# Placing the transposes and the averages of the second attention stage between the two tiles of a block

## The chip, the cores and the metric

The kernel runs on one core of one Trainium2 chip. The metric is the device time of one execution in microseconds (us), as the median of the runs shown. Engines: PE is TensorE, DVE VectorE, ACT ScalarE, POOL GpSimd, SP SyncE, which here issues all DMAs.

## What is computed

Two layers, each an attention block A and a dense block B, with a residual sum around each; 2048 rows of 640 numbers, 32 heads of 20, fp32. The reference, cut to what matters:

```python
def _A_ref(x, wqkv, w_phi, wo):
    q, k, v = split_heads(x @ wqkv)
    pq, pk = q @ w_phi, k @ w_phi                     # per head
    phi_q = concat([softmax(pq), softmax(-pq)])       # 40 features a head
    phi_k = concat([softmax(pk), softmax(-pk)])
    kv = phi_k.T @ v                                  # sum over all rows
    z = phi_k.sum(over rows)
    o = (phi_q @ kv) / (phi_q @ z + 1e-6)
    return merge_heads(o) @ wo
def _B_ref(x, w1, b1, w2):
    h = x @ w1 + b1
    return mish(h) @ w2
for _ in range(2):
    x = x + _A_ref(layernorm(x), ...)
    x = x + _B_ref(layernorm(x), ...)
```

The sum `kv` needs all rows before the first output row can be made. So each layer's attention has two stages.

## The kernel before, in words

The 2048 rows are cut into 8 blocks (NB) of 256 rows, each of two tiles of 128 rows (BT = 2). Products that must be exact in fp32 are made of three products each: every operand is held as a high part and a low part, and high x high, high x low and low x high are added up.

**First stage** (`attend_first`): features of keys and queries and the values of each block; `kv` grows in PSUM over all blocks. The features of the queries are written to DRAM, one tensor `e_d[b]` for each block, turned (L421 to L425), in pieces of 128 bytes; the pieces of the last block are still open when the second stage begins. They sit in a generator, `rest`, and each call of `tail()` (L552) takes one step of it.

**Second stage** (`attend_second`, L547), the one that is changed. For each block b:

- `load(b)` (L517) reads the turned features back: two DMAs of 600 KB into two "big" tiles (L521; there are 5 such buffers) and one of 80 KB into an "ol" tile (L523). In the code after, `phi(b)` does the same.
- `average(b, t)` (L557) makes `o` for tile t: 44 small products on PE (L567) into one `mm_tile` (two PSUM banks; there are two such tiles), then VectorE divides (L576 to L580) into a `row_tile` (tag "xn", 4 buffers).
- `Transposed(rows).all()` (L263) turns the two row tiles of a block: 10 transposes on PE (L278) in three steps, each into a `one_tile` (one PSUM bank; there are four). ScalarE copies the high part out, VectorE subtracts to get the low part (L284).
- `Rows(b, t).half(c, ps)` (L594) is half of the output product `o @ wo` for tile t: 15 products of 320 columns (L342) into the bank `ps`, then VectorE adds the block's input rows x to it (L597) and takes statistics (L598).
- `norm_scale` (L253) makes scale and offset for the layer norm that follows, on GpSimd and VectorE. The block's result, which lies in the tile of x, is stored (L649).
- `fetch(x_src, b + 1)` (L380) reads the next block's x. There are two x tiles.
- `makes[b]` and `fetches[b + 1]` prepare the weights of the dense stage: reads on SP (L141), a copy on ScalarE, a subtraction on GpSimd (L149).

**What sets the order.** For PE and SP the order in this stage is the written one (`manual_schedule`, L605). For the other engines a planner orders the instructions of the whole kernel by its own model of times. Waits between engines come from the use of tiles: a buffer that is given out again waits until its last reader has finished, and two halves written into one `mm_tile` belong to one tile.

**The written order of a block before**, for 1 <= b <= 6: average(b+1, 0); half 0 of tile 0; average(b+1, 1); tail; read of x(b+1); load(b+3); half 1 of tile 0; half 0 of tile 1; transposes of block b+1; half 1 of tile 1; store; reads of weights; tail. Tile 0's halves use one `one_tile` each; tile 1's lie in the two banks of one `mm_tile`, `py`. Ahead of the loop stand the averages of blocks 0 and 1 and loads 1 to 3; in the last block the transposes of the dense stage's first rows (`ahead.all()`) stand in front.

**Dense stage** (`dense`): both products with Mish between them, its PE order made by the planner.

Of the kernel before, what the change touches and what calls it, by code (L numbers as in the profile page):

```python
# [24 lines left out]
BT = 2  # L25
BLK = BT * P
NB = S // BLK
# [15 lines left out]
def kernel(  # L43
# [22 lines left out]
    def mm_tile():  # L66
        return psum.tile([P, 2, 512], F32, tag="mm", name="mm", bufs=2)

    def one_tile():
        return psum.tile([P, 512], F32, tag="one", name="one", bufs=4)  # L70

    def big_tile():
        return work.tile([P, EW], F32, tag="big", name="big", bufs=5)
# [4 lines left out]
    def pair_tile(dtype=F32R):  # L78
        return work.tile([P, 2, BLK], dtype, tag="ol", name="ol", bufs=6)

    def row_block(t, b):
        return t[b * BLK:(b + 1) * BLK, :].rearrange("(p t) d -> p t d", t=BT)
# [211 lines left out]
    def row_tile():  # L294
        return work.tile([P, D], F32, tag="xn", name="xn", bufs=4)
# [40 lines left out]
    def project_half(ps, xts, t, ws, col, c, ks=range(KD)):  # L336
        sl = slice(t * P, (t + 1) * P)
        cs = slice(col + c * HC, col + (c + 1) * HC)
        for k in ks:
            h, l, wh, wl = xts.hs[k], xts.ls[k], ws[k][0][:, cs], ws[k][1][:, cs]  # L340
            for n, (a, r) in enumerate(((h, wh), (h, wl), (l, wh))):
                nc.tensor.matmul(ps[:, :HC], a[:, sl], r, start=(k == 0 and n == 0),  # L342
                                 stop=(k == KD - 1 and n == 2))
# [36 lines left out]
    def fetch(x_src, b, xt=None):  # L380
        xt = x_tile() if xt is None else xt
        nc.sync.dma_start(xt, row_block(x_src, b))
        return xt
# [133 lines left out]
    def load(b):  # L517

        ta, tb, tc_ = big_tile(), big_tile(), pair_tile(F32)
        for t, g0 in ((ta, 0), (tb, 5)):  # L520
            nc.sync.dma_start(t[:120].rearrange("f (g s) -> f g s", s=BLK),  # L521
                              e_d[b][120 * g0:120 * (g0 + 5)].rearrange("(g f) s -> f g s", f=120))
        nc.sync.dma_start(tc_[:80, 0], e_d[b][1200:])  # L523
        return [(ta, tb)[g // 5][:, (g % 5) * BLK:(g % 5 + 1) * BLK] for g in range(10)] + [tc_[:, 0]]

    def finish_kv(kva, kvz, mask):

        acc, acz = row_tile(), row_tile()
        for src, dst, p1, n, w in ((kva, acc, P, 4, 120), (kvz, acz, P, 1, 120), (kvz, acz, 42, 1, 80)):
            c = 120 if w == 80 else 0  # L530
            nc.vector.tensor_tensor(dst[:p1, c:c + n * w].rearrange("p (n w) -> p n w", n=n),
                                    src[:p1, c:c + n * w].rearrange("p (n w) -> p n w", n=n),
                                    mask[:p1, :w].unsqueeze(1).to_broadcast([p1, n, w]), op=ALU.mult)
        yield
        for src, q0, n in ((acc, 0, 4), (acz, 4, 2)):
            ps = one_tile().rearrange("p (n c) -> p n c", n=4)
            for q in range(n):
                p1, w = (P, 120) if q0 + q < 5 else (42, 80)
                nc.tensor.transpose(ps[:w, q, :p1], src[:p1, 120 * q:120 * q + w], ident[:p1, :p1])
            if n == 4:  # L540
                act(kvb[:, :4], ps[:120], AF.Copy)
            else:
                nc.vector.tensor_copy(kvb[:, 4], ps[:120, 0])
                nc.vector.tensor_copy(kvb[:80, 5, :42], ps[:80, 1, :42])
        yield

    def attend_second(x_src, x_dst, acc, fetches, makes, fetch_next, begin_next):  # L547
        kva, kvz, o_ws, loaded, rest = acc
        rows = {}
        div = [None]  # L550

        def tail():  # L552

            with tc.issue_after(div[0]):
                next(rest, None)

        def average(b, t):  # L557

            phs = loaded[b]
            po = mm_tile()  # L560
            for g in range(G):
                n = 120 if g < 10 else 80
                w = GW if g < 10 else 42
                c, j = divmod(g, 8)
                for q in range(2):
                    s0 = t * P + 64 * q
                    nc.tensor.matmul(  # L567
                        po[64 * q:64 * q + 64, c, GW * j:GW * j + w], phs[g][:n, s0:s0 + 64],
                        kvb[:n, g // 2, 64 * (g % 2):64 * (g % 2) + w], start=True, stop=True)
            o = row_tile()  # L570
            den = work.tile([P, H], F32, tag="r", name="den", bufs=2)
            pv = [po[:, c, :(DH + 1) * n].rearrange("p (h d) -> p h d", d=DH + 1)
                  for c, n in ((0, 24), (1, 8))]
            hh = (slice(0, 24), slice(24, H))
            for c in range(2):
                nc.vector.tensor_scalar_add(den[:, hh[c]], pv[c][:, :, DH], DEN_EPS)  # L576
            nc.vector.reciprocal(den, den)
            for c in range(2):
                n = hh[c].stop - hh[c].start
                ins = nc.vector.tensor_tensor(o.rearrange("p (h d) -> p h d", d=DH)[:, hh[c]], pv[c][:, :, :DH],  # L580
                                        den[:, hh[c]].unsqueeze(2).to_broadcast([P, n, DH]), op=ALU.mult)
                div[0] = ins.ins
            rows.setdefault(b, []).append(o)
            if t == BT - 1:
                del loaded[b]

        class Rows:


            def __init__(self, b, t):  # L590
                self.t, self.xt, self.ps = t, xs[b], None
                self.bn = work.tile([P, 2, 6], F32, tag="bn", name="bn", bufs=2)

            def half(self, c, ps):  # L594
                project_half(ps, cur, self.t, o_ws, 0, c)
                part = self.xt[:, self.t, c * HC:(c + 1) * HC]
                nc.vector.tensor_tensor(part, ps[:, :HC], part, op=ALU.add)  # L597
                nc.vector.bn_stats(self.bn[:, c], part)  # L598

            def mean(self):  # L600
                mv = work.tile([P, 2], F32, tag="mv", name="mv", bufs=3)
                nc.vector.bn_aggr(mv, self.bn)
                return mv

        with tc.manual_schedule(engines={mybir.EngineType.PE, mybir.EngineType.SP}):  # L605
            kv = finish_kv(kva, kvz, mask)
            next(rest)
            next(kv)
            loaded[1] = load(1)
            xs = {0: fetch(x_src, 0)}  # L610
            fetches[0]()
            next(rest)
            next(kv)
            next(rest)
            average(0, 0)
            average(0, 1)
            loaded[2] = load(2)
            average(1, 0)
            cur = Transposed(rows.pop(0)).all()
            average(1, 1)  # L620
            loaded[3] = load(3)
            for b in range(NB):
                if b == NB - 1:
                    ahead.all()
                elif b:
                    average(b + 1, 0)
                r0, r1 = Rows(b, 0), Rows(b, 1)
                r0.half(0, one_tile())
                if 0 < b < NB - 1:
                    average(b + 1, 1)  # L630
                tail()
                if b + 1 < NB:
                    xs[b + 1] = fetch(x_src, b + 1)
                if 0 < b and b + 3 < NB:
                    loaded[b + 3] = load(b + 3)
                if b == NB - 3:
                    fetch_next()
                r0.half(1, one_tile())
                mv0 = r0.mean()
                if b == NB - 2:  # L640
                    ahead = begin_next()
                py = mm_tile()
                r1.half(0, py[:, 0])
                if b + 1 < NB:
                    nxt = Transposed(rows.pop(b + 1)).all()
                r1.half(1, py[:, 1])
                norm_scale(b, [mv0, r1.mean()])
                xt = xs.pop(b)
                nc.sync.dma_start(row_block(x_dst, b), xt)  # L649
                makes[b]()  # L650
                if b + 1 < NB:
                    fetches[b + 1]()
                tail()
                if b < NB - 1:
                    cur = nxt
            for _ in rest:
                pass
        return ahead
# [217 lines left out]
```

## Time and profile before

| | |
|---|---|
| median of 3 runs | 1413.73 us (1413.45, 1413.73, 1416.37) |
| the profiled execution | 1414.77 us |
| its span, first to last instruction | 1413.0 us |
| mean granted TensorE clock | 0.999 |
| DMA traffic | 168.05 MB in 348,633 packets, 286,824 of them under 512 B |
| HBM | 103.30 MB read, 62.91 MB written |
| second stage in layer 0, blocks 1 to 7 | from about 292 us to 383 us |
| second stage in layer 1, blocks 1 to 7 | from about 979 us to 1071 us |

How to read the rows of the profile. A row of the chain of waits has start, length and what ran; "x15" is 15 instructions. A row of a timeline has start, length, engine, line of the kernel, operation, tile written and tile read, and in brackets the idle time ahead of it with what ended it. A row of a table by windows has the window, its length, busy time and number of instructions of PE, of PE's weight loads, of DVE, ACT and POOL, then the granted clock, the DMA share and GB/s. A row of a DMA list has the tiles, the number of issues, the size of each and the median time from the issue to the landing. A row of waits has who waited for whom, and in total how long, how often, and the longest. SPq is SP's own queue; times of its rows are those of issuing, not of the transfer.

### The profile page before, as it was taken

The numbers are of one execution on the slowest core, as the hardware profiler recorded it, in microseconds if no ns is written. First come the engines' busy times: TensorE is split into PE (matmuls) and PEld (weight loads), VectorE is DVE, ScalarE is ACT, GpSimd is POOL, SyncE is SP. The second block draws the span as 40 slices with busy tenths as digits, with TensorE's granted clock in tenths as the row PEclk, the third lists the DMA queues.
The fourth block names the chain that finished last, engine by engine and source line by source line (L and its number), as shares of the span: only waits on it lengthen the run. The fifth ranks groups of instructions, "written<-read, shape, count | busy, mean of one in ns | idle before, by whom it ended". The sixth has DMA issues, their size and how long they took to land. (4 is left out here: it accounts for less than half of the span.)

```text
span 1413.0 us, 28124 instructions
## 1 busy us (share of the span) xinstructions
PE 1392.1 (99%) x11528; PEld 1368.6 (97%) x11528; DVE 1076.5 (76%) x1810; ACT 585.1 (41%) x973; POOL 460.3 (33%) x344
## 2 busy tenths in 40 slices
PE   7999999999999999999999999999999999999998
PEld 7999999999999999999999999999999999999998
DVE  4798878685688777788759887887767766767765
ACT  4444343321354445454454333332234444444443
POOL 1354444343442222222234443433434311111112
PEclk9999999999999999999999999999999999999999
DMA  9533422899743322344374434268986212333200
GB/s 307 171 78 59 74 38 39 176 230 245 257 118 94 96 73 67 103 113 94 105 265 85 77 64 71 49 106 216 255 255 212 56 28 87 94 94 94 65 31 19
DMA packets 348633, 168.05 MB, mean 119 GB/s; under 512 B 286824, under 2 KB 322136, under 8 KB 348504
## 3 DMA queue, kind: packets, MB, share of 16 engines
q1 hardware_dynamic: 348504, 166.26, 46.5%
q8 instruction: 90, 1.47, 0.4%
q14 instruction: 39, 0.32, 0.1%
HBM read 103.30 MB, written 62.91 MB: 118 GB/s over the span
## 5 line engine op out<-in xcount | busy, mean ns | idle before, releaser
L717 PE MATMUL mm<-r2h,ol 128*128 128x320 f32 x1280 | 305.7, 310 | 1.5 <-ACT ol L700 1.0
L701 POOL TENSOR_TENSOR ol<-big,ol 128x512 fp32r<-128x512 f32 (+1 forms) x98 | 129.9, 1326 | 457.7 <-ACT ol L700 387.1
L675 PE MATMUL one<-xtl,r1h 128*128 128x256 f32 x960 | 268.8, 280 | 2.0 <-DVE xtl L284 2.0
L675 PE MATMUL one<-xth,r1l 128*128 128x256 f32 x960 | 268.2, 279 | 0.0
L675 PE MATMUL one<-xth,r1h 128*128 128x256 f32 x960 | 266.7, 280 | 0.0
L717 PEld LDWEIGHTS mm<-r2h,ol 128*128 128x128 f32 x1280 | 219.2, 188 | 3.3 <-POOL ol L701 1.7
L717 PE MATMUL mm<-r2l,ol 128*128 128x320 f32 x640 | 197.4, 309 | 0.0
L342 PE MATMUL mm<-r1h,xth 128*128 128x320 f32 x600 | 188.5, 314 | 0.0
L342 PE MATMUL mm<-r1h,xtl 128*128 128x320 f32 x600 | 185.9, 310 | 0.7 <-DVE xtl L284 0.7
L342 PE MATMUL mm<-r1l,xth 128*128 128x320 f32 x600 | 185.8, 310 | 0.0
L675 PEld LDWEIGHTS one<-xtl,r1h 128*128 128x128 f32 x960 | 180.6, 188 | 2.7 <-DVE xtl L284 2.5
L675 PEld LDWEIGHTS one<-xth,r1l 128*128 128x128 f32 x960 | 180.6, 188 | 0.0
L675 PEld LDWEIGHTS one<-xth,r1h 128*128 128x128 f32 x960 | 180.0, 188 | 0.0
L342 PE MATMUL mm<-r2h,xth 128*128 128x320 f32 x460 | 144.3, 314 | 1.0 <-DVE xt L597 1.0
L342 PE MATMUL mm<-r2h,xtl 128*128 128x320 f32 x460 | 142.5, 310 | 0.0
L342 PE MATMUL mm<-r2l,xth 128*128 128x320 f32 x460 | 142.3, 309 | 0.0
L690 DVE TENSOR_SCALAR big<-big 128x512 f32<-128x512 f32 (+1 forms) x98 | 55.9, 571 | 113.3 <-ACT big L688 111.2
L377 POOL TENSOR_TENSOR r<-r,r 128x1280 f32<-128x1280 f32 x32 | 75.7, 2367 | 144.5 <-DVE r L376 141.7
L688 ACT ACTIVATE big<-one,b1s 128x256 f32<-128x256 f32 x192 | 80.7, 468 | 95.9 <-PE one L675 93.7
L717 PEld LDWEIGHTS mm<-r2l,ol 128*128 128x128 f32 x640 | 120.3, 188 | 0.0
L692 ACT ACTIVATE big<-big,two 128x512 f32<-128x512 f32 (+1 forms) x98 | 70.1, 715 | 118.7 <-DVE big L691 116.2
L700 ACT ACTIVATE ol<-big 128x512 fp32r<-128x512 f32 (+1 forms) x98 | 61.0, 622 | 133.7 <-DVE big L699 133.6
(128 smaller groups left out, 3088.4 us busy)
## 6 DMA issues: line engine op xcount, KB each, us to landing
e_d<-r SPq DMA_DIRECT2D x128, 160.0 KB, 4.0
big<-e_d SPq DMA_DIRECT2D x32, 600.0 KB, 9.2
x_d<-xt SPq DMA_DIRECT2D x23, 640.0 KB, 5.6
xt<-x_d SPq DMA_DIRECT2D x22, 640.0 KB, 5.1
n_d<-xn SPq DMA_DIRECT2D x176, 80.0 KB, 2.1
xt<-in_x SPq DMA_DIRECT2D x16, 640.0 KB, 5.8
xn<-x_d SPq DMA_DIRECT2D x28, 320.0 KB, 4.4
v<-n_d SPq DMA_DIRECT2D x30, 256.0 KB, 3.0
```

The lines of the kernel that those rows point to most:

```text
L342: nc.tensor.matmul(ps[:, :HC], a[:, sl], r, start=(k == 0 and n == 0), stop=(k == KD - 1 and n == 2))
L377: nc.gpsimd.tensor_tensor(eg, eg, r.unsqueeze(2).to_broadcast([P, 2 * H, DH]), op=ALU.mult)
L675: nc.tensor.matmul(ph[:, j, :], l, r, start=(n == 0), stop=(n == 3 * KD - 1))
L688: exps[0] = nc.scalar.activation(part(ta, 0)[:, j - js.start], ph[:, j, :], AF.Exp, bias=b1s[:, 2 * pr + j:2 * pr + j + 1]).ins
L690: nc.vector.tensor_scalar_min(e, e, E_CAP)
L692: nc.scalar.activation(r, n, AF.Ln, bias=two)
L700: nc.scalar.activation(ah[:, js], n, AF.Copy)
L701: nc.gpsimd.tensor_tensor(al[:, js], n, ah[:, js].bitcast(F32), op=ALU.subtract)
L717: nc.tensor.matmul(pys[t][:, c, :HC], l[:, j, sl], r, start=(f == 0 and n == 0), stop=(f == KF - 1 and n == 2))
```

## The change

In the loop of the second stage, each block's two averages are made together and no longer with a half of the output product between them. For blocks 2 to 5 they follow the transposes, between the products of tile 0 and those of tile 1, and they are those of block b+2 and no longer of b+1; in blocks 1 and 2 the averages of b+1 stand together ahead of the products (so block 2 has two pairs). The features of block b+4 are read in that same place (in blocks 1 and 2 those of b+3 where they were read before). From block 2 on tile 1's first half follows the transposes too. Tile 1's halves now use a `one_tile` each. Block 2 has one more `tail()`.

```diff
+            def averages(b):
+                for t in range(BT):
+                    average(b, t)
+
+            def phi(b):
+                if b < NB:
+                    loaded[b] = load(b)
+
             for b in range(NB):
                 if b == NB - 1:
                     ahead.all()
-                elif b:
-                    average(b + 1, 0)
+                elif b in (1, 2):
+                    averages(b + 1)
                 r0, r1 = Rows(b, 0), Rows(b, 1)
                 r0.half(0, one_tile())
-                if 0 < b < NB - 1:
-                    average(b + 1, 1)
                 tail()
                 if b + 1 < NB:
                     xs[b + 1] = fetch(x_src, b + 1)
-                if 0 < b and b + 3 < NB:
-                    loaded[b + 3] = load(b + 3)
+                if b in (1, 2):
+                    phi(b + 3)
                 if b == NB - 3:
                     fetch_next()
                 r0.half(1, one_tile())
                 mv0 = r0.mean()
                 if b == NB - 2:
                     ahead = begin_next()
-                py = mm_tile()
-                r1.half(0, py[:, 0])
+                if b < 2:
+                    r1.half(0, one_tile())
                 if b + 1 < NB:
                     nxt = Transposed(rows.pop(b + 1)).all()
-                r1.half(1, py[:, 1])
+                if 2 <= b < NB - 2:
+                    averages(b + 2)
+                    phi(b + 4)
+                if b == 2:
+                    tail()
+                if b >= 2:
+                    r1.half(0, one_tile())
+                r1.half(1, one_tile())
                 norm_scale(b, [mv0, r1.mean()])
```

## What is predicted, and how

> **What bounds the kernel now.** I read the page first, then the chain of work that ended last around one block of the second stage, then the TensorE timeline of the same stage in layer 0, and last the DMA queue (SP's timeline, and the time to landing of single issues).
>
> ```profile
> span 1413.0 us, 28124 instructions
> PE 1392.1 (99%) x11528; PEld 1368.6 (97%) x11528; DVE 1076.5 (76%) x1810; ACT 585.1 (41%) x973; POOL 460.3 (33%) x344
> ```
>
> TensorE is the bound nearly everywhere. So the change is worth what it takes from TensorE's own sequence, less every wait that it puts there. Block 3 of layer 1 in the chain (start, length, what):
>
> ```profile
> 961.81 2.72 PE mm L567 x88
> ...
> 1005.41 1.41 PE mm L567 x44
> 1006.83 2.40 PE one L342 x15
> 1009.23 1.41 PE mm L567 x44
> 1010.64 2.40 PE one L342 x15
> 1013.04 2.20 PE mm L342 x15
> 1015.24 1.09 PE one L278 x10
> 1016.33 2.20 PE mm L342 x15
> 1018.53 1.41 PE mm L567 x44
> ```
>
> A block is average, half, average, half, half, transposes, half: 1018.53 - 1005.41 = 13.12 us without a gap. A half product (L342 x15) takes 2.20 us, but 2.40 behind an average. Two averages back to back (961.81) take 2.72, while two apart take 2 x 1.41 = 2.82. Transposes standing between halves cost 1.09 and nothing beside that.
>
> Layer 0 does the same work with waits. Starts of blocks 2, 4, 5 and 6 (L567), and what stood in front of the late rows (in brackets), from TensorE's timeline:
>
> ```profile
> 305.22 1.38 PE L567 MATMUL mm<-kvb,big 120*64 120x63 f32 x40
> ...
> 331.46 1.39 PE L567 MATMUL mm<-kvb,big 120*64 120x63 f32 x40
> ...
> 342.94 0.42 PE L342 MATMUL mm<-r2h,xth 128*128 128x320 f32 x1 [0.48 <-DVE xt L597]
> ...
> 345.33 1.39 PE L567 MATMUL mm<-kvb,big 120*64 120x63 f32 x40
> ...
> 355.83 1.20 PE L278 MATMUL one<-ident,xn 128*128 128x128 f32 x9 [0.49 <-DVE xn L580]
> 357.59 0.41 PE L342 MATMUL mm<-r2h,xth 128*128 128x320 f32 x1 [0.56 <-DVE xt L597]
> ...
> 359.99 1.39 PE L567 MATMUL mm<-kvb,big 120*64 120x63 f32 x40
> ```
>
> Block 4 takes 345.33 - 331.46 = 13.87 us and block 5 14.66: 0.75 and 1.54 above 13.12, together 2.29. VectorE is late there because the block's input rows x are late. Its first add of block 4 and of block 5:
>
> ```profile
> 337.40 0.49 DVE L597 TENSOR_TENSOR xt<-one,xt 128x320 f32<-128x320 f32 x1 [2.84 <-PE mm L567]
> ...
> 351.89 0.49 DVE L597 TENSOR_TENSOR xt<-one,xt 128x320 f32<-128x320 f32 x1 [3.46 <-issue]
> ```
>
> The rows x arrive over one crowded queue. One stretch of it in layer 1 (issues of SP, then block 3's DMA share in the second-last column, then a wait of SP):
>
> ```profile
> 1006.00 0.34 SPq L649 DMA_DIRECT2D x_d<-xt  x1
> ...
> 1016.18 1.89 SPq L382 DMA_DIRECT2D xt<-x_d  x1
> ...
> 1020.28 0.47 SPq L523 DMA_DIRECT2D ol<-e_d  x1
> 1020.81 0.42 SPq L649 DMA_DIRECT2D x_d<-xt  x1
> ...
> 1030.40 0.33 SPq L382 DMA_DIRECT2D xt<-x_d  x1
> ```
> ```profile
> 1005.34:1018.46 13.12, 13.12 (x159) 12.63 (x158) 9.11 (x25) 1.76 (x4) 4.57 (x4) 1.00 1.02 270
> ```
> ```profile
> SPq L382 <- DMA x_d<-xt: 23.2, 6, 8.4
> ```
>
> The DMA share is 1.02: the engines are full. Only two x tiles exist, so the read of x(b+1) waits until the store of x(b-1) has landed. The landings belonging to the five SP issues above, in their order, each from a window around that issue:
>
> ```profile
> x_d<-xt SPq DMA_DIRECT2D x1, 640.0 KB, 10.1
> ...
> xt<-x_d SPq DMA_DIRECT2D x1, 640.0 KB, 5.9
> ...
> ol<-e_d SPq DMA_DIRECT2D x1, 80.0 KB, 7.9
> ...
> x_d<-xt SPq DMA_DIRECT2D x1, 640.0 KB, 9.5
> ...
> xt<-x_d SPq DMA_DIRECT2D x1, 640.0 KB, 4.1
> ```
>
> So store 2 lands at 1016.1 and x(4) is issued at once. It lands at 1016.18 + 5.9 = 1022.1, and load(6), behind it, ends at 1020.28 + 7.9 = 1028.2. Landings follow the order of issue; one load of features (two reads of 600 KB, one of 80) holds the queue for 1028.2 - 1022.1 = **6.1 us**.
>
> **The change, part by part.** *Fewer visits to the averages.* Blocks 1 to 6 hold twelve single visits in each layer; afterwards there are six double ones (one in block 1, two in block 2, one each in 3 to 5). Two single visits with their dearer halves are 2 x (1.41 + 0.20) = 3.22; a double one is 2.72 + 0.20 = 2.92. Saved: 6 x 0.30 = 1.8 a layer, **3.6 us**. The instructions are the same. That the transposes now lead into averages instead of into a half I take as nothing.
>
> *Single banks for the second tile.* In block 4 of layer 0 the half behind the transposes waited for the add of the half before (342.94, 357.59), since both lay in one tile. That goes for blocks from 2 on: the last half then takes the first transposes' bank, freed a double average and a half (over 5 us) earlier. With it, and with transposes no longer waiting on averages of the same block (355.83), layer 0's **2.3 us** go, if x is in time.
>
> *End of the stage.* The dense stage's first transposes stand right behind block 6:
>
> ```profile
> 1057.74 1.25 PE L278 MATMUL one<-ident,xn 128*128 128x128 f32 x10
> 1059.23 0.38 PE L342 MATMUL one<-r2h,xth 128*128 128x320 f32 x1 [0.24 <-DVE xtl L284]
> ```
>
> They take 1.49 where 1.09 is the work. Block 6's own transposes then lie two halves ahead, so the 0.4 should go; twice, taking layer 0 as equal (an estimate), **0.8 us**.
>
> *DMAs.* SP issues in the written order. Nothing is added in bytes, but load(6) moves from block 3 into block 2, ahead of the store of x(2), and load(7) into block 3. The spill of the last queries, moved up by the additional tail, is ahead of x(4) either way. Before: x(3), load(5), store 2, x(4), load(6). After: x(3), load(5), **load(6)**, store 2, x(4), load(7). So x(4) lands 6.1 us later than now: at 1028.2 in layer 1. SP itself does not wait for load(6)'s buffers: the averages that free them end at about 1003, before SP gets there. For layer 0:
>
> ```profile
> 331.67 1.86 SPq L382 DMA_DIRECT2D xt<-in_x  x1
> ```
> ```profile
> xt<-in_x SPq DMA_DIRECT2D x1, 640.0 KB, 5.6
> ```
>
> 337.3 now, 343.4 then.
>
> *When x is needed.* This is the added wait. Of the four single banks, a block from 2 on uses the first two for tile 0's halves, and the third transposes take the first bank again. They wait until VectorE has added x to the first half. Now an average, two halves and an average separate that half from the transposes; afterwards one half. A block without averages is 4 x 2.20 + 1.09 = 9.89. In layer 1, block 2 starts at 1005.41 - 13.12 - 0.30 = 991.99 (one merge in block 1), block 3 at 991.99 + 9.89 + 2 x 2.92 = 1007.72, block 4 at 1007.72 + 9.89 + 2.92 = 1020.53. Its third transposes are due 2 x 2.20 + 0.87 (eight of ten transposes) later, at 1025.8. The add is through 0.6 after the landing (0.49, and 0.1 until it starts, 337.3 to 337.40): 1028.8. **Wait 3.0 us.** In layer 0: 305.22 - 0.30 = 304.92, then 320.65, 333.46, due 338.7, ready 344.0. **Wait 5.3 us.** Behind it on TensorE stand the averages and both halves of tile 1; on VectorE, behind the add, the second add, the statistics and the low parts of the transposes, which have some 5 us until the last half.
>
> Block 5 is next: x(5) follows load(7) (6.1), store 3 (1020.81 + 9.5 - 1028.2 = 2.1) and its own 4.1: 1028.2 + 12.3 = 1040.5, added at 1041.1. The third transposes are due at 1028.8 + 12.81 = 1041.6. In time by 0.5, and the same sum in layer 0 gives 356.3 against 356.8. Block 4 has no load, so the queue then recovers.
>
> *Sum:* -3.6 - 2.3 - 0.8 + 3.0 + 5.3 = **+1.6 us**. The profiled execution took 1414.77 (span 1413.0 and 1.8 around it), so 1416.4 on its own time; it lies 1.04 above the median of 1413.73. Against the median: **1415.3 us**.
>
> *Unknown.* The planner orders ACT, VectorE and GpSimd anew. I take that at nothing, the row it is nearest to being layer 1's gapless 13.12; its ends are layer 0's 1.54 in each of four late blocks (+6.2) and a gain of no more than the 6.7 counted above without the waits.
>
> The Trainium skill prices a transfer otherwise (DMA: Bandwidth & Descriptors, Anatomy of one DMA): a fixed 2.0 us, and bytes at 436 GB/s. By that a load of 1.31 MB holds the queue for 3.0 us, as an estimate, and the waits would be nothing and 2.2. The trace has 6.1 for the same load, so the row stands.
>
> **Rivals.** *A, the queue is kinder* (x is in time because load(6) is partly hidden). For it: block 5 and 6 of layer 1 run now without a gap although the queue is full. Against it: landings in issue order at a DMA share of 1.02. Then the waits for x go, but the averages in block 3 need load(5) (block 4 now). In layer 0 its two reads are issued at 318.14,
>
> ```profile
> 318.14 1.24 SPq L521 DMA_DIRECT2D big<-e_d  x2
> ```
> ```profile
> big<-e_d SPq DMA_DIRECT2D x2, 600.0 KB, 9.5
> ```
>
> which lands them at some 328 to 329, needed at 320.65 + 4.40 + 1.09 + 0.65 = 326.8: 1 to 3 us. Result -6.7 + 1 to 3: 1408 to 1410. (In the forecast this wait lies inside the 5.3.) The page's 3.0 us gives -6.7 + 2.2, about 1409, by that rule the same case.
>
> *B, late x holds VectorE for longer* (slower). Place: VectorE's in-order queue from the first add of blocks 4 and 5. Layer 0 shows it now: with x landing 2 us behind its half the block lost 0.75, at 5 us 1.54, and layer 1, where the add is not late, lost nothing. So it decides from about 2 us of lateness, and afterwards x(4) is 5 to 8 us behind its half. Against it: the instructions behind the add have 3 to 5 us until TensorE needs them. Price 0.75 to 1.54 in two blocks of two layers, 3.0 to 6.2 more: 1418.3 to 1421.5.
>
> *C, the clock drops in the wait.* Every window quoted shows 1.00 granted, but none has a gap of 3 us. If some 3.4 us of work behind each wait ran at half speed, that would add 3.4 a layer at most (1.5 halves twice as long), 3.4 if it happens in layer 0 alone: 1418.7. The Trainium skill (TensorE: Matmul & The Clock Gate, HAM oscillation) has idle gaps over about 3.4 us bringing the half clock; no run here shows it.
>
> That the order doesn't come about is excluded: TensorE's and SP's are written by hand in this stage.
>
> **How the numbers follow.** Forecast 0.50 (its own range 1412.5 to 1418), A 0.20, B 0.25, C 0.05. A measurement of this kernel can tell about 0.2% (2.8 us) from no change. Faster than 1410.9 is most of A: 0.17. Slower than 1416.6 is B, C and the upper part of the forecast: 0.40. Within: 0.43. The range takes in the forecast and about half of A and B: 1409.5 to 1420.
>
> **What would show it.** Double averages of 2.72, and blocks 3 to 5 at 12.8 us where nothing is late; in block 4 a wait of TensorE in the third transposes, about 3 us in layer 1 and, with block 3's wait for load(5), 5 in layer 0, released by L597; x(4) landing near 343 and 1028. It is wrong if x(4) lands before 339 and 1026 (A), if more than 1 us is lost behind the transposes (B), or if PEclk falls (C).

## The result, and the profile after

The changed kernel takes 1420.95 us (median of 6 runs, 1420.29 to 1424.72); the kernel before, run beside it, 1415.04 us (6 runs, 1413.45 to 1416.8). The ratio is 1.005, 95% interval 1.0039 to 1.0061: slower by 0.5%, more than the 0.2% that can be told apart, and above the range. The profiled execution has a span of 1419.2 us against 1413.0, so 6.2 us more, at a mean granted clock of 0.998.

The page of the changed kernel. TensorE's busy time is nearly that of before (1392.1): what the pairs save and what a slower clock adds about cancel, so the longer span shows as idle time.

```profile
span 1419.2 us, 28117 instructions
PE 1391.4 (98%) x11528; PEld 1371.2 (97%) x11528; DVE 1074.0 (76%) x1810; ACT 586.6 (41%) x973; POOL 460.3 (32%) x344
```

Most of what is lost lies in blocks 3 and 4 of the second stage, in both layers. Where nothing waits, the pairs save what was forecast. The chain of the changed kernel shows it (start, length, what): the transposes of one block, a double average of 2.70, and the transposes of the next block.

```profile
1046.08 1.09 PE one L278 x10
1047.17 2.70 PE mm L567 x88
...
1058.87 1.09 PE one L278 x10
```

From transposes to transposes a block takes 1058.87 - 1046.08 = 12.79 us, with nothing idle (13.12 before). Now layer 0, TensorE's timeline. What to look at is the distance between the starts, beside 1.18 for ten transposes that lead into averages and 2.70 for a double average. In brackets stands the idle time ahead of a row; the distances lose a little more than that.

```profile
325.56 1.25 PE L278 MATMUL one<-ident,xn 128*128 128x128 f32 x10
326.74 0.80 PE L567 MATMUL mm<-kvb,big 120*64 120x63 f32 x20
329.11 0.80 PE L567 MATMUL mm<-kvb,big 120*64 120x63 f32 x20 [1.56 <-DMA big<-e_d]
...
331.22 0.41 PE L342 MATMUL one<-r2h,xth 128*128 128x320 f32 x1
...
340.13 1.03 PE L278 MATMUL one<-ident,xn 128*128 128x128 f32 x8
342.92 0.44 PE L278 MATMUL one<-ident,xn 128*128 128x128 f32 x2 [1.76 <-DVE xt L597]
343.29 1.94 PE L567 MATMUL mm<-kvb,big 120*64 120x63 f32 x40
...
347.53 0.41 PE L342 MATMUL one<-r2h,xth 128*128 128x320 f32 x1
```

The averages in block 3 wait for load(5): 331.22 - 326.74 = 4.48, so **1.78 us** over 2.70. The third transposes of block 4 wait for the add of x: 343.29 - 340.13 = 3.16, **1.98** over 1.18. Then the averages take 347.53 - 343.29 = 4.24 although nothing is late for them, **1.54** over 2.70. Layer 1:

```profile
1012.79 1.25 PE L278 MATMUL one<-ident,xn 128*128 128x128 f32 x10
1015.30 0.80 PE L567 MATMUL mm<-kvb,big 120*64 120x63 f32 x20 [1.26 <-DMA big<-e_d]
1018.30 0.80 PE L567 MATMUL mm<-kvb,big 120*64 120x63 f32 x20 [2.19 <-DMA big<-e_d]
1019.02 1.81 PE L567 MATMUL mm<-kvb,big 120*64 120x63 f32 x40
...
1024.23 0.31 PE L342 MATMUL one<-r2h,xth 128*128 128x320 f32 x1
...
1030.83 1.03 PE L278 MATMUL one<-ident,xn 128*128 128x128 f32 x8
1032.95 0.44 PE L278 MATMUL one<-ident,xn 128*128 128x128 f32 x2 [1.09 <-DVE xt L597]
1033.32 1.39 PE L567 MATMUL mm<-kvb,big 120*64 120x63 f32 x40
1034.62 1.36 PE L567 MATMUL mm<-kvb,big 120*64 120x63 f32 x40
1037.01 0.41 PE L342 MATMUL one<-r2h,xth 128*128 128x320 f32 x1 [0.92 <-DVE xt L597]
```

Here load(5) holds block 3 up twice. From the transposes' start to the second average 1019.02 - 1012.79 = 6.23 instead of 1.18 + 1.30: **3.75**. The second average and the half behind it (1024.23 - 1019.02 = 5.21 for 1.39 + 2.31) are slow by **1.51**, the third transposes of block 4 wait **1.31**, and tile 1's first half comes **1.0** late (2.39 for 1.39).

The slow stretches without a wait are the clock. The tables by windows (granted clock in the third column from the right), first layer 0, then layer 1:

```profile
343.20:345.20 2.00, 2.00 (x47) 1.92 (x46) 0.07 (x1) 0.39 (x1) 1.73 (x3) 0.67 1.00 193
345.20:347.60 2.40, 2.40 (x51) 2.35 (x47) 2.37 (x8) 0.00 (x0) 0.12 (x1) 0.56 1.09 248
1019.00:1021.00 2.00, 2.00 (x53) 1.92 (x49) 1.49 (x5) 0.00 (x0) 0.00 (x0) 0.68 1.07 215
1021.00:1022.40 1.40, 1.40 (x7) 1.40 (x6) 1.27 (x5) 0.00 (x0) 0.00 (x0) 0.50 1.07 217
1022.40:1025.00 2.60, 2.60 (x17) 2.60 (x17) 0.76 (x3) 0.00 (x0) 0.00 (x0) 0.86 1.21 264
```

If the clock is either whole or half, it was at half for 2 x (0.33 x 2.00 + 0.44 x 2.40) = 3.4 us in layer 0 and 2 x (0.32 x 2.00 + 0.50 x 1.40 + 0.14 x 2.60) = 3.4 us in layer 1.

What made the 1.0 us late at 1037.01 stands in the chain of the changed kernel:

```profile
1008.20 10.05 DMA big<-e_d
...
1021.84 7.96 DMA raw<-in_w
...
1029.83 1.50 ACT r1h L116
...
1031.40 3.44 POOL r1l L149
...
1035.93 0.23 DVE stats L260 x2
...
1036.56 0.40 DVE xt L597
```

A weight read, issued at 1021.84 behind load(6) and store 2, keeps GpSimd in the dense stage's L149; the scale of the layer norm (L258) queues behind that, VectorE stands at L260 for the scale, and behind L260 stands the add that frees TensorE's bank. SP's timeline, last, before and after:

```profile
994.52 8.02 SPq L425 DMA_DIRECT2D e_d<-r  x4
...
1003.34 1.23 SPq L521 DMA_DIRECT2D big<-e_d  x2
```
```profile
995.50 10.89 SPq L425 DMA_DIRECT2D e_d<-r  x4
...
1007.15 1.38 SPq L521 DMA_DIRECT2D big<-e_d  x2
```

Load(5) of layer 1 is issued 3.8 us later than before, mostly because the four spills of the first stage's last queries ahead of it take 2.9 us longer to issue; yet the averages that use it start at 1012.79 + 1.18 = 1013.97, where the kernel before started them at 1018.53. Its last DMA took as long as before from issue to landing, 10.2 us against 9.9; here the row of before:

```profile
1004.62 0.95 SPq L523 DMA_DIRECT2D ol<-e_d  x1
```
```profile
ol<-e_d SPq DMA_DIRECT2D x1, 80.0 KB, 9.9
```

So it landed at 1014.5 before, and at 1018.8 now.

### The profile page after: what moved, and what is told of

It reads as the page before. It is cut to its first block, busy times and chain, and to the rows that moved or that the text cites. A ratio compares the mean times of both kernels' runs of the same rounds, so it can differ in the third digit from the quotient of the medians.

```text
span 1419.2 us, 28117 instructions
## 1 busy us (share of the span) xinstructions
PE 1391.4 (98%) x11528; PEld 1371.2 (97%) x11528; DVE 1074.0 (76%) x1810; ACT 586.6 (41%) x973; POOL 460.3 (32%) x344
## 5 line engine op out<-in xcount | busy, mean ns | idle before, releaser
L342 PE MATMUL mm<-r1h,xth 128*128 128x320 f32 x600 | 188.4, 314 | 0.0
L342 PE MATMUL mm<-r1h,xtl 128*128 128x320 f32 x600 | 185.7, 310 | 0.7 <-DVE xtl L284 0.7
L342 PE MATMUL mm<-r1l,xth 128*128 128x320 f32 x600 | 185.6, 309 | 0.0
L342 PEld LDWEIGHTS mm<-r1h,xth 128*128 128x128 f32 x600 | 112.8, 188 | 2.0
L342 PEld LDWEIGHTS mm<-r1h,xtl 128*128 128x128 f32 x600 | 112.8, 188 | 1.1 <-DVE xtl L284 1.0
L342 PEld LDWEIGHTS mm<-r1l,xth 128*128 128x128 f32 x600 | 112.8, 188 | 0.0
```

## The experiments

Ratios are to the kernel before on the same chip (its median 1415.97, 1415.87 and 1415.83 in the three groups, e1 to e4, e5 to e8, e9 to e12).

**e1_again: the changed kernel once more, no edit**, to see which waits are of the order and which of one execution.

> The changed kernel once more, to see which of its waits return. Theory Q (load(6) stands ahead of the store of x(2) in a full DMA queue, so x(4) is late in both layers): x(4) lands near 342 us in layer 0 and 1029 to 1032 in layer 1, TensorE waits 1 to 2 us in block 4's third transposes in both layers, and the granted clock halves for 3.4 us once in each layer (about 1.5 us each). Rival L (layer 1's additional lateness, x(3) landing 3 us later than the queue's order explains, was chance of one execution): x(3) lands near 1009 in layer 1, the wait of 1.3 us in block 3's transposes is gone, and the span is some 3 us shorter than 1419.2. Ratio to before 1.005 by Q, 1.003 by L.

1422.1 us, ratio 1.0043 (1.003 to 1.0056). In layer 1 load(5) costs 2.1 us of waiting and x(4) 2.7, at whole clock; in layer 0 the clock falls once:

```profile
325.00:350.00 25.00, 21.01 (x273) 20.04 (x272) 10.73 (x31) 4.32 (x7) 4.58 (x5) 0.93 0.99 239
1012.00:1042.00 30.00, 24.08 (x304) 23.14 (x303) 14.12 (x44) 4.21 (x7) 5.59 (x7) 1.00 0.98 249
```

So the places are the same in both executions, and the shares of load, x and clock shift between them. Rival L is out: in layer 1 x(3) is issued at 1007.80 and lands 5.7 us later, at 1013.5 and not near 1009, and the span is no shorter (1420.6). Late x(3) and load(5) in layer 1 belong to the changed order and were no chance of one execution: the four spills ahead of them take 9.9 to 10.9 us to issue in all seven profiles of the changed kernel and its variants (e1, e4, e6, e9, e11, e12), and 8.0 in the kernel before. In layer 0 there is no such difference (7.9 to 10.5, and 9.8 before).

**e2_pairs_only: the kernel before with the two averages together**, ahead of the products.

```diff
                 elif b:
                     average(b + 1, 0)
+                    average(b + 1, 1)
                 r0, r1 = Rows(b, 0), Rows(b, 1)
                 r0.half(0, one_tile())
-                if 0 < b < NB - 1:
-                    average(b + 1, 1)
```

> The kernel before with one part of the change alone: both averages of block b+1 stand together ahead of block b's products, for blocks 1 to 6. Transposes, banks, loads and tails are as before. Theory Q: the pairs are worth what the prediction counted, 0.30 us for each of six in two layers, 3.6 us, and nothing is late because the DMAs keep their order: ratio 0.9975, clock at 1.00 throughout. Rival V (pairs burden VectorE, which has to divide two tiles in a row, and the kernel gets slower by that): waits of TensorE for VectorE's L580 or L597 of over 1 us in several blocks, ratio 1.000 or above.

1415.27 us, 0.9991 (0.9982 to 1.0): less than 3.6 us come out. The profile of layer 0 shows why (waits of VectorE and of TensorE's weight loads, with their total, number and longest):

```profile
DVE stats L260 <- POOL stats L258: 12.5, 4, 5.5
...
PEld mm L342 <- DVE xt L597: 2.0, 2, 1.7
```

VectorE stands 12.5 us at L260 for GpSimd, and TensorE behind VectorE. Block 5 there takes 363.73 - 347.03 = 16.7 us, 3.9 more than 12.79, and 1.5 of these are a half product at a lower clock. A second loss, in both layers, is 0.5 us in block 1 and 0.35 in block 2: the pair takes both `mm_tile`s, and waits for the add that frees `py`. The single banks of the whole change take that one away.

**e3_pairs_and_place: e2, and tile 1's halves behind the transposes, in single banks**; loads as before.

```diff
-                py = mm_tile()
-                r1.half(0, py[:, 0])
+                if b < 2:
+                    r1.half(0, one_tile())
                 if b + 1 < NB:
                     nxt = Transposed(rows.pop(b + 1)).all()
-                r1.half(1, py[:, 1])
+                if b >= 2:
+                    r1.half(0, one_tile())
+                r1.half(1, one_tile())
```

> As the run with the pairs alone, and in addition the transposes of block b+1 stand between the products of tile 0 and of tile 1, which use single banks (for blocks 2 to 6, and single banks in all). Averages are of block b+1, and the loads are in the order of before. Theory Q: the place itself costs little. The third transposes are due 8.2 us behind a block's start in place of 10.4, so layer 0's x(5), landing near 352, may hold them by up to 1 us; ratio 0.997 to 0.999. Rival P (the new place of the transposes, which takes the bank of the first half again after a single half, is what makes late x cost): waits of 1 us and over in the third transposes of blocks 3 to 5, ratio above 1.001.

1420.09 us, 1.0026 (1.0017 to 1.0036), 4.8 us above e2. The wait is not the one that the rival names: TensorE's transposes wait for the averages' quotient (L580), in layer 0

```profile
PEld one L278 <- DVE xn L580: 3.9, 3, 3.1
```

since VectorE stands 14.5 us at L260 there. So the place alone, without the moved loads, costs time; e8 shows that L260 is a part of the cause and not the whole.

**e4_loads_back: the changed kernel with load(b+3) in its old place**, behind the read of x(b+1).

```diff
-                if b in (1, 2):
+                if 0 < b and b + 3 < NB:
                     phi(b + 3)
...
                     averages(b + 2)
-                    phi(b + 4)
```

> The changed kernel with the loads put back: load(b+3) behind the read of x(b+1) in blocks 1 to 4, as before, and no load behind the averages. Theory Q: x(4) lands near 337 us in layer 0 and 1022 to 1025 in layer 1, and TensorE doesn't wait for it in block 4's transposes. But the averages of block 6, made in block 4, then wait for load(6): up to 3.6 us in layer 0 and 1 to 4 in layer 1, so the time is between 1.000 and 1.005 of before. Rival P (the place of the transposes, and not load(6), makes x late): the wait of block 4's third transposes for L597 stays at 1 to 2 us.

1417.93 us, 1.0014 (1.0005 to 1.0024). x(4) is back at 337.0 and 1026.7, and no transposes wait for x. What is left is the loads, in layer 0

```profile
PE mm L567 <- DMA big<-e_d: 3.6, 3, 1.4
```

and 3.5 us in layer 1, and the clock falls in both layers. This order is 4.2 us faster than e1 and 2 us slower than the kernel before. The order of loads and x decides who is late and by how much; with whole loads, neither order tried fits averages a block earlier.

**The split.** The next four make the layer norm's offset in this stage on GpSimd (two negations and a product), so that L260 on VectorE falls away there; elsewhere it stays. Later lines move by 6 (L603 is L597, L573 is L567, L284 is L278, L290 is L284, L348 is L342). The edit, cut:

```diff
-    def norm_scale(b, mvs):
+    def norm_scale(b, mvs, pool=False):
...
+        if pool:
+            neg = work.tile([P, BT], F32, tag="neg", name="neg", bufs=2)
+            for t in range(BT):
+                nc.gpsimd.tensor_scalar(neg[:, t:t + 1], mvs[t][:, 0:1], -1.0, 1.0, op0=ALU.mult, op1=ALU.mult)
+            nc.gpsimd.tensor_tensor(stats[:, b, 1], neg, stats[:, b, 0], op=ALU.mult)
+            return
...
-                norm_scale(b, [mv0, r1.mean()])
+                norm_scale(b, [mv0, r1.mean()], True)
```

**e5_before_split: the kernel before with the split.**

> The kernel before, where in the second stage GpSimd makes the whole of norm_scale (scale and offset), so that VectorE never waits for GpSimd there (L260 falls away; the offset is made by two small operations and a product on GpSimd). Theory G (late weights hold GpSimd at L149, GpSimd holds the scale, and VectorE, which waits for it at L260 in its own order, holds the divisions and adds that TensorE needs): layer 0's blocks 4 and 5 lose less than now (13.87 and 14.66 us against 13.12), at least 1 us in all, and no wait of VectorE for L258 remains; ratio 0.998 to 0.9995. Rival Q (late x alone makes those waits): they remain, ratio 1.000.

1414.7 us, 0.9995 (0.9986 to 1.0004). Layer 0's waits of 2.3 us shrink to 0.2, yet the median moves by less than can be told. The first add of block 4, in layer 0:

```profile
339.35 0.49 DVE L603 TENSOR_TENSOR xt<-one,xt 128x320 f32<-128x320 f32 x1 [3.73 <-issue]
```

Block 4 starts at 332.51 here, so this add comes 6.8 us into it, against 337.40 - 331.46 = 5.9 before, and yet the block takes 13.37 us and not 13.87. So late x alone did not make block 4's wait; it took L260 in VectorE's order as well. For block 5 this is not shown, as x(5) was also earlier.

**e6_after_split: the changed kernel with the split.**

> The changed kernel with the same: no wait of VectorE for GpSimd in the second stage. Theory G: the 1.0 to 1.2 us at the head of tile 1's half in block 4 (released by L597, behind L260) go in both layers, so 1 to 2.4 us of the kernel's 6; the waits for load(5) in block 3 and for x(4) in block 4's third transposes remain, and the halved clock may. Ratio to before 1.002 to 1.004. Rival Q (all comes from x and the loads): nothing moves, 1.0045.

1425.33 us, 1.0068 (1.0053 to 1.0082): not faster than without it, but slower, a miss. The wait behind L260 is gone, and x and load(5) take its place; layer 0:

```profile
PE one L284 <- DVE xt L603: 3.1, 2, 2.0
```

The longer wait for the add is in block 5: x(5), which the prediction had in time by 0.5, lands at 360.1 (355.2 in the first profile of the changed kernel), because each read of x from x(3) on is issued 2.9 to 3.5 us later. That is not the split's doing: e1, without an edit, issues x(4) and x(5) as late (340.63 and 354.81; here 340.66 and 354.85). Without the wait behind L260, block 5 comes to its transposes 0.9 us sooner than in e1 (357.73, and 358.59), and meets the late x(5) there. So the order has no slack for x(5) either. What else makes e6 slower than e1 stays open.

**e7_pairs_split: e2 with the split.**

> Pairs alone (both averages of block b+1 ahead of block b's products), with no wait of VectorE for GpSimd. Theory G: the 3.6 us that the pairs save are seen, because what took them in the run with pairs alone (block 5 of layer 0, about 3.8 us with the halved clock, behind waits of VectorE for L258 of up to 5.5 us) is gone; ratio 0.996 to 0.9975. Rival V (pairs themselves burden VectorE): ratio 0.999 or above, with waits of TensorE for L580 or L597.

**1411.78 us, 0.9972 (0.9963 to 0.9981)**, the fastest version that computes the whole result. Its chain in layer 1 has no gap from the pair in block 2 on, until the end of the stage (1028.62 - 1018.52 = 10.10, the sum of four halves and the transposes, 9.89, and the 0.20 by which a half behind averages is dearer):

```profile
1018.52 4.60 PE one L348 x30
1023.12 2.20 PE mm L348 x15
...
1028.62 2.70 PE mm L573 x88
```

With the split on both sides, the pairs give 1414.70 - 1411.78 = 2.9 us of the 3.6 forecast; block 1's pair still waits 0.5 us for `py` in each layer. And with the pairs on both sides, taking L260 out of VectorE's order gives 1415.27 - 1411.78 = 3.5 us.

**e8_pairs_place_split: e3 with the split.**

> Pairs and the transposes between the tiles with single banks, with no wait of VectorE for GpSimd. Theory G: the waits of the transposes for L580 (3 to 4 us in block 4 of each layer) go, since the divisions stood behind L260; ratio 0.996 to 0.998, close to the run with the pairs alone and this. Rival P (the place of the transposes itself makes late x cost): the third transposes wait for L597 by 1 us and over in several blocks, ratio above 1.000.

1415.13 us, 0.9998 (0.9989 to 1.0007): 5 us better than e3, but still 3.4 worse than e7, so most of the place's cost is not L260's. The transposes no longer wait for L580; in block 6 a half waits for the low parts of the transposes right in front of it, 1.4 us in layer 1 and in layer 0

```profile
PE one L348 <- DVE xtl L290: 1.5, 1, 1.5
```

In the whole change two averages stand between them in blocks 2 to 5, and block 6 has no averages ahead; there this wait does not come up.

**e9_after_short_loads: the changed kernel with load(5) and load(6) cut to a fifth** (without the split; later lines move by 1; the edit, cut).

```diff
+            n = 1 if b in (5, 6) else 5
-            nc.sync.dma_start(t[:120].rearrange("f (g s) -> f g s", s=BLK),
-                              e_d[b][120 * g0:120 * (g0 + 5)].rearrange("(g f) s -> f g s", f=120))
+            nc.sync.dma_start(t[:120, :n * BLK].rearrange("f (g s) -> f g s", s=BLK),
+                              e_d[b][120 * g0:120 * (g0 + n)].rearrange("(g f) s -> f g s", f=120))
...
-        return [(ta, tb)[g // 5][:, (g % 5) * BLK:(g % 5 + 1) * BLK] for g in range(10)] + [tc_[:, 0]]
+        return [(ta, tb)[g // 5][:, (g % 5 % n) * BLK:(g % 5 % n + 1) * BLK] for g in range(10)] + [tc_[:, 0]]
```

> The changed kernel, but of the features of blocks 5 and 6 only the first fifth is read (2 x 120 KB and 80 KB for 2 x 600 KB and 80 KB), and the averages of these two blocks use that fifth five times over; every instruction of the engines stays. It takes away 1 MB from the queue in each of load(5) and load(6), nothing else. Theory Q (the change loses its time to the full queue: load(5) late for the earlier averages, x(4) behind load(6), the weights behind both, and the half clock after those gaps): all of these go, 1.78 + 1.98 + 1.55 in layer 0 and 3.75 + 1.51 + 1.30 + 0.99 in layer 1, 12.9 us: about 1408 (1406.5 to 1410), no wait over 0.5 us in blocks 3 and 4, clock 1.00 there. Rival V (the cost lies in the order of VectorE and GpSimd that the new place brings, whatever the queue does): the waits of L260 for GpSimd's L258 stay at 2 to 3 us and TensorE goes on losing 2 to 4 us in blocks 4 to 6, 1414 to 1418.

1409.56 us, 0.9958 (0.9946 to 0.997), inside Q's range. TensorE is busy without a break and the clock whole where 3.3 and 5.5 us were idle in the changed kernel:

```profile
325.00:350.00 25.00, 25.00 (x314) 24.55 (x313) 17.38 (x50) 6.00 (x10) 8.97 (x10) 1.00 0.84 248
1012.00:1042.00 30.00, 30.00 (x389) 29.50 (x384) 21.35 (x64) 8.80 (x14) 13.69 (x13) 1.00 0.81 260
```

**e10_before_short_loads: the same cut in the kernel before.**

> The kernel before with the same cut of load(5) and load(6); the averages of blocks 5 and 6 use the fifth that is read. Theory Q: of the kernel before only layer 0's 2.3 us of waits hang on the queue, so about 1412.7 (1411.5 to 1414), and the difference to the changed kernel with the same cut is the gain that the change has where transfers cost little: 3.6 for the pairs and up to 0.8 at the end of the stage, 3.6 to 4.4 us in the change's favour. Rival V: the difference is under 1 us or against the change.

1413.23 us, 0.9982 (0.9973 to 0.999). This lies in Q's range too, and TensorE's old waits in layer 0 are gone from its profile. The difference to e9 is 3.7 us for the change, against 5.9 us the other way with whole loads: what decides is the time that load(5) and load(6) take in the queue. V is out.

**e11_after_short_load6: the cut in load(6) alone**, `n = 1 if b in (6,) else 5`.

> The changed kernel with load(6) alone cut to a fifth (the averages of block 6 use that fifth five times over); load(5) is whole. Theory Q: x(4) lands some 5 us earlier, about 337 and 1027, so the waits in block 4's third transposes go (1.98 and 1.30), with them the clock drop of layer 0 that followed (1.55) and about 1 us behind late weights in layer 1, while the averages of block 3 go on waiting for load(5), 1.8 to 2.3 us in layer 0 and 2.3 to 3.8 in layer 1: about 1415.2 (1413.5 to 1417). Rival S (x(4) is late through the store of x(2), which takes 10 us, and not through load(6)): x(4) lands after 340 and 1030 as now and the time stays within 1 us of the changed kernel, 1420 to 1422.

1417.29 us, 1.0009 (0.9997 to 1.0021), spread from 1411.2 to 1421.6, 0.3 above Q's range. The wait for x(4) is gone in both layers, as Q has it. In layer 1 x(4) lands at 1026.7; in layer 0 its first add, at 341.91, waits for TensorE and not for x. Load(5) costs more than Q took in layer 0 and about what it took in layer 1 (in this order below), and in both the clock falls to half behind it (0.84 from 327 to 338, 0.76 from 1017 to 1024):

```profile
PE mm L568 <- DMA big<-e_d: 3.3, 2, 2.6
```
```profile
PE mm L568 <- DMA big<-e_d: 2.4, 1, 2.4
```

**e12_after_filled_gaps: spare work where TensorE waited.**

```diff
-                if b + 1 < NB:
+                if b in (3, 4):
+                    nxt = Transposed(rows.pop(b + 1))
+                    nxt.step()
+                    nxt.step()
+                    spare = mm_tile()
+                    project_half(spare[:, 0], cur, 0, o_ws, 0, 0)
+                    nxt.all()
+                elif b + 1 < NB:
```

> The changed kernel with one spare half product (15 matmuls, 2.2 us, its result unread) between the second and the third step of the transposes in blocks 3 and 4 of each layer, so that TensorE is busy where it waited. It adds 4 x 2.2 = 8.8 us of work. Theory H (the half clock comes from the gaps of about 2 us): the spare work lies in the waits (1.78 and about 1.6 of 2.2 in layer 0; 2.2 and 1.3 in layer 1), so it costs 8.8 - 6.9 = about 2 us, the granted clock stays at 1.00 in blocks 3 and 4 of both layers, and the clock's 3.1 us are saved: 1419 to 1421. Rival W (the half clock comes from something else, for instance from the transposes or the start of the averages): the clock still falls to half for some 3.4 us in block 4 of layer 0 and block 3 of layer 1, and the kernel is at 1422 to 1424.

1422.25 us, 1.005 (1.0038 to 1.0063): 1.3 us over the changed kernel for 8.8 us of more work, but 1.25 above H's range and inside W's. The clock's part came out as H has it: 1.00 in both stretches, where the changed kernel has 0.93 and 0.94. The mean clock of whole executions says the same: 0.999 to 1.000 in the six runs here, 0.997 to 0.998 in the six of the changed kernel.

```profile
325.00:350.00 25.00, 24.73 (x309) 23.82 (x308) 11.57 (x34) 4.31 (x7) 4.76 (x5) 1.00 1.01 247
1012.00:1042.00 30.00, 28.28 (x334) 27.61 (x333) 14.09 (x44) 4.31 (x7) 5.75 (x8) 1.00 0.99 254
```
```profile
325.00:350.00 25.00, 21.68 (x278) 20.86 (x278) 12.98 (x39) 4.32 (x7) 4.71 (x5) 0.93 1.01 259
1012.00:1042.00 30.00, 24.53 (x297) 23.56 (x296) 15.16 (x46) 4.32 (x7) 4.71 (x5) 0.94 0.99 251
```

The miss in time is a wait for x(5) in block 5 of layer 0, 1.9 us. x(5) comes as late as in e1 (its add starts at 358.96 in both), and block 5 reaches its transposes 1.8 us sooner than there (356.83, and 358.59).

## Why the prediction was wrong, step by step

Two steps failed: the wait for load(5) in layer 1, which was put at nothing, and the fall of the clock behind short waits, which got a chance of 0.05. By the prediction's own terms:

- **Pairs, -3.6: right.** 12.79 a block where 12.80 was said. In time, e5 against e7 gives 2.9 (with block 1's wait for `py` left in e7), and e10 against e9 gives 3.7 with the end of the stage.
- **Layer 0's old waits, -2.3: right in number, and the reading behind it half right.** None of them is in the changed kernel's layer 0. But the prediction put them down to late x alone, and e5 has x(4) later still and 0.5 of block 4's 0.75 gone, with L260 taken away.
- **End of the stage, -0.8: nearly.** The transposes in block 6, the dense stage's first ones and three halves among them take 9.27 us before and 8.97 after, 0.3 less in each layer and 0.6 in all: the dense stage's transposes fell from 1.49 to 1.01, while two halves there got dearer (2.36 and 2.31).
- **x(4) later by one load: right in kind.** In layer 1 load(6) lands 5.8 us behind load(5) (1011.77 + 12.8, and 1008.58 + 10.2); 6.1 was said. The Trainium skill's fit, which gave 3.0 (DMA: Bandwidth & Descriptors, Anatomy of one DMA), is stated there for DMAs that GpSimd issues, and all of these are SP's. x(4) lands at 342.3 (343.4 was said) and at 1032.3 (1028.2; the queue had been 3.8 us late since load(5)). With e4 and e11, where x(4) is early and its wait gone, the cause is shown.
- **Waits for x(4) and load(5): this step failed in layer 1.** Layer 0 has 1.78 + 1.98 = 3.8 (5.3 was said), so 1.5 less. For layer 1 the prediction gave 3.0 to x(4) and nothing to load(5). Measured were 1.3 and 3.75, 2.05 more. "Needed at 326.8" was worked out for layer 0 in rival A, and not for layer 1, where load(5) landed at 1014.5 even before and the averages that use it were to start at 1007.72 + 4.40 + 1.09 = 1013.2. That check would have given some 1 us; the rest is that load(5) is issued 3.8 us later in the changed kernel, which the prediction, taking SP's times from before, had no term for.
- **Rival C, 0.05: this was the larger error.** The half clock came in both layers and cost 1.54 + 1.51 = 3.05 us. The step that failed is "none has a gap of 3 us", which made some 3 us the condition: the idle times here were 1.6 and 1.8 in layer 0 and 1.3 and 2.2 close together in layer 1. Even by that condition the chance was too small, since the forecast itself had a wait of 5.3 us in layer 0. The price was near by luck: 3.4 for one layer was said, taking 3.4 us of work to run twice as long; measured were 3.4 us of time at half clock, 1.5 us lost, in two layers.
- **Rival B, 0.25: the place right, the cause another.** VectorE's queue held the add in block 4, and it cost 1.0 us in layer 1 (1.1 and 1.0 in the two layers of e1), where 0.75 to 1.54 in each of four blocks was said. Not late x held it: late weights held GpSimd, GpSimd held L260, and L260 the add.

The sum by measured terms: -3.6 - 2.3 - 0.6 + 3.76 + 1.54 + 3.75 + 1.51 + 1.31 + 1.0 = +6.4, for 6.2 in the spans. The forecast's +1.6 lacks 4.8, of which 3.05 is the clock, 1.0 rival B, 0.5 the loads and x (2.05 - 1.5), and 0.2 the end of the stage. So the forecast and two of its rivals happened together, and the range, which took them as alternatives and half of B only, was too narrow upward by 1 us. That the miss is as large as 1 us is chance in part: the range was counted from a kernel before of 1413.73, and the six runs beside the change gave 1415.04; from 1413.73 the measured 5.9 us would end at 1419.6. The failed steps are the same either way. What stays open is why the spills of layer 1 take 2 to 3 us longer to issue in the changed order.

## What to carry to other kernels

When work is moved ahead, compute for each of its inputs, in every pass of the loop, the landing against the new due time; in a queue at a DMA share of 1.0, a read that is moved ahead makes another late, and who is late has its price (e4's order was 4.2 us faster than e1's). Short gaps on TensorE cost more than their length, since the clock may halve behind them. Where a gain in one engine's sequence doesn't show, look for an instruction on a helper engine that waits for another helper (VectorE's L260 for GpSimd): taking it out gave 3.5 us with the pairs (e7) and 5 with the place (e8), but less than can be told in the kernel before (e5) and nothing in the changed kernel (e6), where the queue was the limit.

## What the runs showed of the hardware

- The clock falls to half after gaps of about 2 us, for 3.4 us of time, and not each time. In the changed kernel's layer 0, idle times of 1.6 and 1.8 us, 14 us apart, were enough; in e1's layer 1 TensorE was idle for 2.1 and then 2.7 us, and in e3's layer 0 for 2.9, at a granted clock of 1.00. The length is the same wherever it fell: worked out in the same way, e1, e2, e3, e6 and e11 have 3.4 to 3.5 us. The Trainium skill (TensorE: Matmul & The Clock Gate, What's actually happening) has a free-running window of 3413 ns, and the 3.4 us agree with it; its rule of no gaps over about 3.4 us (HAM oscillation) is too lenient for this case. That the phase of the window decides would fit, but no run here shows it.
- SP's issuing itself takes longer when the queue is full. In the changed kernel, at a DMA share of 1.0, the store of x(2) took 5.29 us to issue at 326.69 and 5.73 at 1016.01, where others in the same stretch take 0.3 to 0.5. With load(5) and load(6) cut to a fifth (e9), the same store took 0.34 in both layers.
